# Quarter tiles for every attention product, source order on every queue, early loads on three queues

## The chip, the cores and the metric

The kernel runs on one core of one Trainium2 chip. The metric is device time in microseconds. The kernel before took 952.7 us, the median of three runs (951.31 to 954.98); one further execution was profiled, and every view below comes from it.

## The reference

Sigmoid attention over 8 batches, 12 heads, 448 positions and 64 values per head, then a top-1 mixture of experts over the 3584 tokens of 768 values (8 experts, 768 to 1024 to 768, fp32 throughout):

```python
def _attn_ref(q, k, v):                      # each (8, 12, 448, 64)
    scores = scale * np.matmul(q, k.transpose(0, 1, 3, 2)) - np.log(S)
    attn = 1.0 / (1.0 + np.exp(-scores))
    return np.matmul(attn, v)
...
x = attn_out.transpose(0, 2, 1, 3).reshape(B * S, H * D)      # (3584, 768)
def _moe_ref(x, w_gate, w1, w2):             # w1 (8, 768, 1024), w2 (8, 1024, 768)
    logits = x @ w_gate
    expert_idx = np.argmax(logits, axis=1)
    probs = softmax(logits)                  # sum + 1e-9
    gate_w = probs[np.arange(N), expert_idx]
    for e in range(E):
        mask = expert_idx == e
        h = np.maximum(x[mask] @ w1[e], 0.0)
        out[mask] = gate_w[mask, None] * (h @ w2[e])
```

## The kernel before

**Attention.** Two heads make a pair `g`, 6 pairs a batch, 48 in all. `load_pair` brings k and q of a pair in eight strided DMAs (32 partitions each), `turn` transposes them on VectorE (`kt`, `qt`: the two heads on partitions 0 to 63 and 64 to 127). `load_values` brings v. The 448 keys of a head are cut into three chunks of 128 keys and a rest of 64. For a chunk of 128, `scores` issues one matmul per head into a PSUM tile of its own (64 rows of the array by 128 columns: halves, line 492), `squash` turns each tile into sigmoids on ScalarE (line 478), and `weighted` multiplies them by v (128 rows by 64 columns: halves the other way, line 515). The rests of two pairs are put together: four matmuls on the four 64x64 quarters of the array (lines 500 and 524), the two heads of a pair into the two halves of one PSUM tile. Seven steps (3 + 3 chunks and one step of rests) do two pairs, so there are 168 steps. At each even step, called a visit here, TensorE does the value products of the two steps before (with exceptions at the ends of two pairs) and then the scores of two new steps. `xh` and `xl` (lines 530 and 531) take a finished pair out of PSUM as a sum of two parts.

**Experts.** The most frequent expert of each batch is applied to the whole batch in place (`moe`), with fp32 as a sum of two parts in three matmuls: 288 matmuls of 128x128 by 448 columns a batch (lines 208 and 229). `ps_moe` has two buffers, which the gate's small products share. `Weights.load` brings w1 in 8 and w2 in 6 tiles a batch (`wst`, five buffers), `part_split` makes the two parts of each: a cast on ScalarE (line 143) and a subtraction on GpSimd, called POOL (line 144). Tokens that chose another expert are done at the end, item by item, from `x_tok` and the records `recs` in DRAM.

**The mixture of both.** From step 33 on, 14 expert matmuls are written behind each step. The gate of a batch (`gate_a` to `gate_e`, `load_regs`) runs in steps 3 to 9 after the batch's attention; `tokens` writes `x_tok` in two halves through one buffer `xt` (lines 399 to 404), so the first transpose of the second half waits until the first half is written.

**Order.** Within `attention`, `manual_schedule(engines={ET.PE})` keeps TensorE's instructions in source order; VectorE and ScalarE are kept in source order only up to step 3. All else is ordered by a scheduler that works on a modelled time. Every queue executes in its order, and an instruction that waits holds what is behind it. After the attention the scheduler orders everything, in both kernels.

Of the kernel before, what the change touches and what calls it, by code (L numbers as in the profile page):

```python
# [25 lines left out]
def tile_sigmoid_attention_top1_moe(  # L26
# [78 lines left out]

    def setup():
        wg = const.tile([P, KD, E], F32, name="wg")
        nc.sync.dma_start(wg, w_gate.rearrange("(t p) e -> p t e", p=P))
        nc.scalar.copy(wgs[:, :, 0:E], wg)
# [152 lines left out]
    def gate_b(b):  # L262
# [29 lines left out]
        s1 = tl("s1")  # L292
        nc.scalar.activation(s1, z, AF.Sigmoid)
        s2 = tl("s2")
        nc.scalar.activation(s2, z, AF.Sigmoid, scale=-1.0)
        return oh, s1, s2

    def gate_c(b, oh, s1, s2):
# [121 lines left out]
    KC, KB = 3, 3 * P  # L420
# [24 lines left out]
    def load_values(g):  # L445
# [4 lines left out]
        t = apool.tile([P, 2, KC, D], F32, tag="vn", bufs=3, name=f"vn_{g}")  # L450
        eng.dma_start(t, v[b, 2 * hp : 2 * hp + 2, :KB].rearrange("h (p c) d -> p h c d", c=KC))
        e = apool.tile([P, D], F32, tag="ve", bufs=4, name=f"ve_{g}")
        for h in range(2):
            eng.dma_start(e[quarter(g, h)], v[b, 2 * hp + h, KB:, :])
        ops[g, "v"] = (t, e)

    def turn(g, nm):
# [15 lines left out]
    ST = 2 * KC + 1  # L473
    N_ST = NG // 2 * ST

    def squash(g, c, h, ps):
# [1 line left out]
        nc.scalar.activation(at, ps[:, :S], AF.Sigmoid, bias=bias_s, scale=SCALE)  # L478
# [5 lines left out]
    def scores(s):  # L484
        u, i = divmod(s, ST)
        n, c = divmod(i, KC)
        if n < 2:
            g = 2 * u + n
            pss = [score_tile(f"{g}_{c}_{h}") for h in range(2)]
            for h in range(2):  # L490
                ks = ops[g, "k"][OWN[h], :KB].rearrange("d (p c) -> d c p", c=KC)[:, c]
                nc.tensor.matmul(pss[h][:, :S], ks, ops[g, "q"][OWN[h]], start=True, stop=True)  # L492
            for h in range(2):
                squash(g, c, h, pss[h])
        else:
            pss = [score_tile(f"{2 * u + n}_{KC}") for n in range(2)]
            for n in range(2):
                g = 2 * u + n
                for h in range(2):
                    nc.tensor.matmul(  # L500
                        pss[n][quarter(g, h), :S], ops[g, "k"][OWN[h], KB:], ops[g, "q"][OWN[h]],
                        start=True, stop=True,
                    )
            for n in range(2):
                squash(2 * u + n, KC, 0, pss[n])

    def weighted(s):
        u, i = divmod(s, ST)
        n, c = divmod(i, KC)
        if n < 2:  # L510
            g = 2 * u + n
            if c == 0:
                psv[g] = ps_av.tile([P, 512], F32, tag="av", name=f"av_{g}")
            for h in range(2):
                nc.tensor.matmul(  # L515
                    psv[g][OWN[h], :S], ops[g, "v"][0][:, h, c, :], ats.pop((g, c, h)), start=(c == 0), stop=False
                )
            return
        for n in range(2):
            g = 2 * u + n  # L520
            at = ats.pop((g, KC, 0))
            for h in range(2):
                rows = quarter(g, h)
                nc.tensor.matmul(psv[g][OWN[h], :S], ops[g, "v"][1][rows], at[rows], start=False, stop=True)  # L524
        for n in range(2):
            g = 2 * u + n
            pv = psv.pop(g)
            xh = xpool.tile([P, S], F32R, tag="xh", name=f"xh_{g}")
            xl = xpool.tile([P, S], F32R, tag="xl", name=f"xl_{g}")
            nc.scalar.copy(xh, pv[:, :S])  # L530
            nc.vector.tensor_sub(xl, pv[:, :S], xh.bitcast(F32))  # L531
            xch[divmod(g, NP)] = (xh, xl)
# [4 lines left out]
    ET = mybir.EngineType
    ORDERED_TO = 3
# [382 lines left out]
```

## Time and profile before

| | |
|---|---|
| median of 3 runs | 952.7 us (951.31 to 954.98) |
| profiled execution, its own time | 959.16 us |
| its span, first to last instruction | 957.4 us |
| TensorE busy | 897.4 us (94%) |
| GpSimd (POOL), ScalarE (ACT), VectorE (DVE) busy | 407.2, 385.7, 350.1 us |
| mean granted TensorE clock | 0.970 |
| DMA | 120.47 MB, 319250 packets, of them 222596 under 512 B |
| first matmul of attention, first expert matmul | 8.06 us, 96.70 us |

How to read it: TensorE shows as PE (matmuls) and PEld (weight loads, which overlap them). A row of the timeline has a start, a length, an engine, a line, an operation with output and inputs, a count, and in brackets the idle time before it and what ended that. SPq, ACTq and POOLq are the queues on which SyncE, ScalarE and GpSimd issue DMAs. Matmuls are pipelined, so lengths of single matmuls overlap, and distances from start to start say more than lengths.

### The profile page before, as it was taken

The page shows a single profiled execution, that of the slowest core. Times are in us where ns is not written, and L with a number is a line of the kernel's source. Part 1 is how long each engine was busy: PE and PEld are TensorE (multiplying, and loading weights), DVE is VectorE, ACT ScalarE, POOL GpSimd, SP SyncE. Part 2 cuts the span into 40 slices and gives each one's busy share as a digit, 9 for nine tenths or more (in the row PEclk, how much of TensorE's full clock was granted, in tenths as well). Part 3 has the DMA queues.
Part 4 walks back from the last instruction along what each step waited for, and adds up shares of the span by engine and source line. Part 5 has one row for each costly group of instructions (what it writes and reads, how often), then busy time and mean ns, then how long its engine had stood idle before and what let it go on. Part 6 is the DMA issues. An engine that isn't in the chain of part 4 may idle for free.

```text
span 957.4 us, 13357 instructions
## 1 busy us (share of the span) xinstructions
PE 897.4 (94%) x4470; PEld 624.7 (65%) x4470; DVE 350.1 (37%) x730; ACT 385.7 (40%) x690; POOL 407.2 (43%) x362
## 2 busy tenths in 40 slices
PE   9778999999999999997999999999999999997986
PEld 5223667666656767665766766767666678996786
DVE  3335333621352324621334323513352325136354
ACT  4444453325233443343333633435343532313344
POOL 3002431835056523653047613743255508967130
PEclk9778999999999999998999999999999999998898
DMA  9667862755437653955347653946353405529414
GB/s 128 118 121 173 163 155 55 184 122 161 79 90 148 134 137 65 190 100 158 59 112 146 153 116 75 201 106 149 60 150 91 139 1 147 161 56 301 148 43 140
DMA packets 319250, 120.47 MB, mean 126 GB/s; under 512 B 222596, under 2 KB 314212, under 8 KB 319184
## 3 DMA queue, kind: packets, MB, share of 16 engines
q1 hardware_dynamic: 310512, 106.34, 48.2%
q0 software_dynamic: 6816, 13.07, 5.5%
q8 instruction: 35, 0.57, 0.3%
q10 hardware_dynamic: 1856, 0.23, 0.2%
q14 instruction: 31, 0.25, 0.1%
HBM read 97.55 MB, written 24.64 MB: 128 GB/s over the span
## 4 chain that ended last, share of the span: by engine, by line
PE 53%; DMA 7%; DVE 3%; issue 2%; ACT 2%; SPq 1%; POOL 1%; POOLq 0%; DVEq 0%; ACTq 0%
PE ps L229 18%; PE ps L208 12%; PE av L515 6%; PE sc L492 6%; PE ps L797 6%; DMA wst<-in_moe_w_dram 5%; PE psg L256 1%; PE sc L500 1%; PE av L524 1%; DMA x_tok<-xt 1%; DMA w2r<-in_moe_w_dram 1%; DMA w1r<-in_moe_w_dram 1%; SPq L439 1%; POOL w2l L144 0%; ACT w2h L143 0%
## 5 line engine op out<-in xcount | busy, mean ns | idle before, releaser
L478 ACT ACTIVATE at<-sc,bias_s 128x448 f32<-128x448 f32 x336 | 187.6, 636 | 234.9 <-PE sc L492 208.2
L144 POOL TENSOR_TENSOR w2l<-wst,w2h 128x512 fp32r<-128x512 f32 x96 | 123.9, 1307 | 279.1 <-ACT w2h L143 217.6
L144 POOL TENSOR_TENSOR w1l<-wst,w1h 128x768 fp32r<-128x768 f32 x64 | 117.2, 1841 | 158.5 <-ACT w1h L143 157.7
L229 PE MATMUL ps<-hh,w2h 128*128 128x448 f32 x384 | 144.1, 375 | 7.4 <-DVE gt L381 2.7
L208 PE MATMUL ps<-xh,w1h 128*128 128x448 f32 x384 | 142.9, 372 | 8.0 <-DVE hl L214 8.0
L492 PE MATMUL sc<-qt,kt 64*128 64x448 f32 x576 | 141.4, 598 | 5.8 <-ACT at L478 5.3
L515 PE MATMUL av<-at,vn 128*64 128x448 f32 x576 | 134.7, 582 | 12.2 <-DVE xl L531 11.1
L229 PE MATMUL ps<-hl,w2h 128*128 128x448 f32 x384 | 143.4, 373 | 0.0
L229 PE MATMUL ps<-hh,w2l 128*128 128x448 f32 x384 | 142.1, 370 | 0.6 <-POOL w2l L144 0.6
L208 PE MATMUL ps<-xl,w1h 128*128 128x448 f32 x384 | 142.1, 370 | 0.0
L208 PE MATMUL ps<-xh,w1l 128*128 128x448 f32 x384 | 141.8, 369 | 0.0
L492 PEld LDWEIGHTS sc<-qt,kt 64*128 64x128 f32 x576 | 67.7, 254 | 84.1 <-issue 63.1
L214 DVE SCALAR_TENSOR_TENSOR hl<-ps,hh 128x448 fp32r<-128x448 f32 x64 | 39.8, 622 | 196.6 <-ACT hh L213 196.6
L143 ACT CAST w2h<-wst 128x512 fp32r<-128x512 f32 x96 | 57.6, 621 | 99.4 <-PE ps L229 58.7
L229 PEld LDWEIGHTS ps<-hh,w2h 128*128 128x128 f32 x384 | 75.0, 195 | 21.4 <-issue 9.0
L208 PEld LDWEIGHTS ps<-xh,w1h 128*128 128x128 f32 x384 | 72.3, 188 | 23.6 <-DVE hl L214 10.0
L515 PEld LDWEIGHTS av<-at,vn 128*64 128x64 f32 x576 | 37.4, 142 | 76.5 <-issue 52.0
L229 PEld LDWEIGHTS ps<-hh,w2l 128*128 128x128 f32 x384 | 75.0, 195 | 12.0 <-issue 5.5
L229 PEld LDWEIGHTS ps<-hl,w2h 128*128 128x128 f32 x384 | 75.0, 195 | 9.7 <-issue 6.2
L143 ACT CAST w1h<-wst 128x768 fp32r<-128x768 f32 x64 | 53.5, 836 | 68.8 <-DMA wst<-in_moe_w_dram 25.1
L208 PEld LDWEIGHTS ps<-xh,w1l 128*128 128x128 f32 x384 | 72.1, 188 | 13.2 <-issue 7.5
L208 PEld LDWEIGHTS ps<-xl,w1h 128*128 128x128 f32 x384 | 72.4, 189 | 12.6 <-issue 7.1
(148 smaller groups left out, 907.7 us busy)
## 6 DMA issues: line engine op xcount, KB each, us to landing
wst<-in_moe_w_dram SPq DMA_DIRECT2D x64, 384.0 KB
wst<-in_moe_w_dram SPq DMA_DIRECT2D x48, 512.0 KB
kn<-in_k_dram SPq DMA_DIRECT2D x192, 56.0 KB
x_tok<-xt SPq DMA_DIRECT2D x64, 168.0 KB
out_dram<-ob POOLq DMA_DIRECT2D x96, 112.0 KB, 3.2
qn<-in_q_dram SPq DMA_DIRECT2D x188, 56.0 KB
vn<-in_v_dram SPq DMA_DIRECT2D x45, 192.0 KB
w1r<-in_moe_w_dram SPq DMA_DIRECT2D x12, 512.0 KB
```

The costliest lines, as they stand in the source:

```text
L143: nc.scalar.copy(hi, st)
L144: eng.tensor_tensor(lo, st, hi.bitcast(F32), op=ALU.subtract)
L208: nc.tensor.matmul(ps[:, :S], a[:, ws], b_, start=(t == 0 and n == 0), stop=(t == KD - 1 and n == 2))
L214: nc.vector.scalar_tensor_tensor(hl[:, :S], ps[:, :S], 0.0, hh[:, :S].bitcast(F32), op0=ALU.max, op1=ALU.subtract)
L229: nc.tensor.matmul(ps[:, :S], a, b_, start=(j == 0 and n == 0), stop=(j == KF - 1 and n == 2))
L256: nc.tensor.matmul(psg[: 2 * E, :S], wgs[:, t], xch[b, t][n], start=(t == 0 and n == 0), stop=(t == KD - 1 and n == 1),)
L439: eng.dma_start(t[32 * a : 32 * (a + 1)], src[b, 2 * hp + h, :, 32 * f : 32 * (f + 1)].rearrange("(j r) s -> r j s", r=32),)
L478: nc.scalar.activation(at, ps[:, :S], AF.Sigmoid, bias=bias_s, scale=SCALE)
L492: nc.tensor.matmul(pss[h][:, :S], ks, ops[g, "q"][OWN[h]], start=True, stop=True)
L500: nc.tensor.matmul(pss[n][quarter(g, h), :S], ops[g, "k"][OWN[h], KB:], ops[g, "q"][OWN[h]], start=True, stop=True,)
L515: nc.tensor.matmul(psv[g][OWN[h], :S], ops[g, "v"][0][:, h, c, :], ats.pop((g, c, h)), start=(c == 0), stop=False)
L797: nc.tensor.matmul(*a, **kw)
```

## The change

Every attention product becomes a quarter. The 448 keys of a head are cut into seven chunks of 64 (`KC = S // DK`). A step takes one chunk of two pairs: four score matmuls on the four quarters into two PSUM tiles, two sigmoids, and later four value matmuls on the quarters. Seven steps still do two pairs. v of a pair comes in two DMAs, one per head, with seven consecutive keys on a partition.

All engines, and the queues of DMAs with them, are in source order while the attention lasts. The order of loads and transposes within seven steps (`READY`) is rewritten, `kt`, `qt` and `vn` have four buffers where they had three. The first expert's weights are loaded where they were, but cast at step 32 (`ahead(0)`, then `ahead(2)`).

Loads: q of pairs 0 and 1 on ScalarE's queue (before: pair 0), v of pairs 0 to 9 on POOL's (before: 0 to 2), the gate weights and the blank of `recs` on POOL's (before: SP's). The gate weights' cast and subtraction move from ScalarE and VectorE to POOL. The gate's two small sigmoids move from `gate_b` to `gate_c`, one step later.

```diff
+    wg = const.tile([P, KD, E], F32, name="wg")
     def setup():
-        nc.sync.dma_start(wg, w_gate.rearrange("(t p) e -> p t e", p=P))
-        nc.scalar.copy(wgs[:, :, 0:E], wg)
-        nc.vector.tensor_sub(wgs[:, :, E : 2 * E], wg, wgs[:, :, 0:E].bitcast(F32))
+        nc.gpsimd.tensor_copy(wgs[:, :, 0:E], wg)
+        nc.gpsimd.tensor_sub(wgs[:, :, E : 2 * E], wg, wgs[:, :, 0:E].bitcast(F32))
...
-        nc.sync.dma_start(recs.rearrange("(p r) w -> p r w", p=P), blank3)
+        nc.gpsimd.dma_start(recs.rearrange("(p r) w -> p r w", p=P), blank3)
...
-    KC, KB = 3, 3 * P
+    DK = P // 2
+    KC = S // DK
...
-            eng = nc.scalar if (g, nm) == (0, "q") else nc.sync
+            eng = nc.scalar if g < Q_ACT and nm == "q" else nc.sync
...
-        t = apool.tile([P, 2, KC, D], F32, tag="vn", bufs=3, name=f"vn_{g}")
-        eng.dma_start(t, v[b, 2 * hp : 2 * hp + 2, :KB].rearrange("h (p c) d -> p h c d", c=KC))
-        e = apool.tile([P, D], F32, tag="ve", bufs=4, name=f"ve_{g}")
+        t = apool.tile([P, KC, D], F32, tag="vn", bufs=4, name=f"vn_{g}")
         for h in range(2):
-            eng.dma_start(e[quarter(g, h)], v[b, 2 * hp + h, KB:, :])
-        ops[g, "v"] = (t, e)
+            eng.dma_start(t[quarter(g, h)], v[b, 2 * hp + h].rearrange("(p c) d -> p c d", c=KC))
+        ops[g, "v"] = t
...
     def scores(s):
+        u, c = divmod(s, ST)
+        two = [2 * u + n for n in range(2)]
+        pss = [score_tile(f"{g}_{c}") for g in two]
+        for g, ps in zip(two, pss):
             for h in range(2):
+                ks = ops[g, "k"][OWN[h]].rearrange("d (p c) -> d c p", c=KC)[:, c]
+                nc.tensor.matmul(ps[quarter(g, h), :S], ks, ops[g, "q"][OWN[h]], start=True, stop=True)
+        for g, ps in zip(two, pss):
+            squash(g, c, ps)
...
-    WARM, V_POOL = 76, 3
+    WARM, V_POOL, Q_ACT = 76, 10, 2
...
     READY = {
-        0: lambda u: (turn(2 * u + 1, "k"), load_values(2 * u + 1)),
-        1: lambda u: turn(2 * u + 1, "q"),
-        2: lambda u: load_pair(2 * u + 5),
-        4: lambda u: (turn(2 * u + 2, "k"), load_values(2 * u + 2)),
-        5: lambda u: (turn(2 * u + 2, "q"), load_pair(2 * u + 6)),
+        0: lambda u: (turn(2 * u + 2, "k"), load_pair(2 * u + 4)),
+        1: lambda u: (turn(2 * u + 2, "q"), load_values(2 * u + 2)),
+        3: lambda u: (turn(2 * u + 3, "k"), load_pair(2 * u + 5)),
+        4: lambda u: (turn(2 * u + 3, "q"), load_values(2 * u + 3)),
     }
...
-        order.enter_context(tc.manual_schedule(engines={ET.PE}))
-        first = order.enter_context(ExitStack())
-        first.enter_context(tc.manual_schedule(engines={ET.DVE, ET.Activation}))
+        order.enter_context(tc.manual_schedule())
...
+            if s == START - 1:
+                wts.ahead(2)
...
-                        wts.ahead(2)
+                        wts.ahead(0)
```

Three places show what moves. On TensorE, early in the attention before, around the first step of rests: `sc` rows of 128x448 are halves, `sc` rows of 64x448 quarters, `av` rows from `vn` halves and from `ve` quarters.

```order
L515 MATMUL av_368<-at_0_0_306,vn_284 64x448
L515 MATMUL av_368<-at_0_1_308,vn_284 64x448
L515 MATMUL av_368<-at_1_0_329,vn_284 64x448
L515 MATMUL av_368<-at_1_1_331,vn_284 64x448
L500 MATMUL sc_3_373<-qt_229,kt_227 64x448 x2
L500 MATMUL sc_3_374<-qt_289,kt_282 64x448 x2
L492 MATMUL sc_0_0_383<-qt_348,kt_341 128x448
L492 MATMUL sc_0_1_384<-qt_348,kt_341 128x448
```

The same place in the changed kernel: a visit of two value steps and two score steps.

```order
L503 MATMUL av_298<-at_1_277,vn_230 64x448 x2
L503 MATMUL av_301<-at_1_279,vn_237 64x448 x2
L503 MATMUL av_298<-at_2_310,vn_230 64x448 x2
L503 MATMUL av_301<-at_2_312,vn_237 64x448 x2
L490 MATMUL sc_4_344<-qt_228,kt_226 64x448 x2
L490 MATMUL sc_4_345<-qt_235,kt_233 64x448 x2
L490 MATMUL sc_5_354<-qt_228,kt_226 64x448 x2
L490 MATMUL sc_5_355<-qt_235,kt_233 64x448 x2
```

Three shapes in a visit have become one. On ScalarE before, at the place of the gate weights and then at that of the first expert's weights (`at` are sigmoids, `xh` copies of finished pairs, `w1h` casts):

```order
L478 ACTIVATE at_2_0_424<-sc_2_0_420,bias_s 128x448
L109 CAST wgs<-wg 128x6x8
L478 ACTIVATE at_2_1_426<-sc_2_1_421,bias_s 128x448
...
L143 CAST w1h_0_853<-wst_0_843 128x768
L530 CAST xh_903<-av_684 128x448
L530 CAST xh_907<-av_752 128x448
L143 CAST w1h_1_859<-wst_1_845 128x768
L478 ACTIVATE at_2_0_915<-sc_2_0_911,bias_s 128x448
```

and the changed kernel's ScalarE at the first expert's weights:

```order
L511 CAST xh_975<-av_740 128x448
L511 CAST xh_979<-av_743 128x448
L477 ACTIVATE at_2_989<-sc_2_983,bias_s 128x448
L477 ACTIVATE at_2_991<-sc_2_984,bias_s 128x448
L477 ACTIVATE at_3_999<-sc_3_993,bias_s 128x448
L477 ACTIVATE at_3_1001<-sc_3_994,bias_s 128x448
L143 CAST w1h_0_1025<-wst_0_924 128x768
L143 CAST w1h_1_1031<-wst_1_926 128x768
```

The cast of the gate weights has left ScalarE, and the copies of the finished pairs stand ahead of the first expert cast. On VectorE before, `xf` and `xt` are the token transposes of batch 0, and `xt_1` opens the second half:

```order
L399 TENSOR_TENSOR xf_1_0_1064<-xh_540,xl_541 128x448
L462 STREAM_TRANSPOSE kt_635<-kn_430 128x448
L462 STREAM_TRANSPOSE qt_672<-qn_435 128x448
L462 STREAM_TRANSPOSE kt_719<-kn_493 128x448
L462 STREAM_TRANSPOSE qt_773<-qn_498 128x448
L400 STREAM_TRANSPOSE xt_1_1063<-xf_1_0_1064 128x14x32
L531 TENSOR_TENSOR xl_649<-av_570,xh_648 128x448
```

and in the changed kernel, where `hl` is the second part of the first expert's hidden values:

```order
L399 STREAM_TRANSPOSE xt_0_1021<-xf_0_2_1093 128x14x32
L214 SCALAR_TENSOR_TENSOR hl_0_1144<-ps_0_0_1085,hh_0_1143 128x448
L398 TENSOR_TENSOR xf_1_0_1158<-xh_584,xl_585 128x448
L399 STREAM_TRANSPOSE xt_1_1157<-xf_1_0_1158 128x14x32
L461 STREAM_TRANSPOSE kt_1175<-kn_905 128x448
L398 TENSOR_TENSOR xf_1_1_1187<-xh_707,xl_708 128x448
L399 STREAM_TRANSPOSE xt_1_1157<-xf_1_1_1187 128x14x32
L214 SCALAR_TENSOR_TENSOR hl_0_1144<-ps_0_1_1153,hh_0_1143 128x448
```

The tokens of batch 0 have moved from the first stage to steps 31 to 36, among the first expert's hidden values.

More of the change, by code (lines that the diff above doesn't have):

```diff
@@ L104, in tile_sigmoid_attention_top1_moe @@
     wgs = const.tile([P, KD, 2 * E], F32R, name="wgs")
+    wg = const.tile([P, KD, E], F32, name="wg")
     def setup():
-        wg = const.tile([P, KD, E], F32, name="wg")
-        nc.sync.dma_start(wg, w_gate.rearrange("(t p) e -> p t e", p=P))
-        nc.scalar.copy(wgs[:, :, 0:E], wg)
-        nc.vector.tensor_sub(wgs[:, :, E : 2 * E], wg, wgs[:, :, 0:E].bitcast(F32))
+        nc.gpsimd.tensor_copy(wgs[:, :, 0:E], wg)
+        nc.gpsimd.tensor_sub(wgs[:, :, E : 2 * E], wg, wgs[:, :, 0:E].bitcast(F32))
         blank = wpool.tile([P, 1024], U32, tag="wst", bufs=RAWS_AHEAD, name="blank")
@@ L291, in gate_b, with gate_c @@
         nc.vector.tensor_tensor(z, lg, bc(mx), op=ALU.subtract)
[L292 to L298, printed above, removed]
+        return oh, z
+    def gate_c(b, oh, z):
         def tl(nm, shape, dt=F32):
             return small.tile(shape, dt, tag=nm, name=f"{nm}_{b}")
+        s1, s2 = tl("s1", [P, NCH, E]), tl("s2", [P, NCH, E])
+        nc.scalar.activation(s1, z, AF.Sigmoid)
+        nc.scalar.activation(s2, z, AF.Sigmoid, scale=-1.0)
         pc = small_ps(b, "pc")
@@ L460, in turn @@
             return
-        t = apool.tile([P, S], F32, tag=nm + "t", bufs=3, name=f"{nm}t_{g}")
+        t = apool.tile([P, S], F32, tag=nm + "t", bufs=4, name=f"{nm}t_{g}")
         nc.vector.transpose(t, ops.pop((g, nm + "n")).rearrange("p j s -> p (j s)"))
@@ L471, in tile_sigmoid_attention_top1_moe, with squash @@
     ats, psv = {}, {}
-    ST = 2 * KC + 1
+    ST = KC
     N_ST = NG // 2 * ST
-    def squash(g, c, h, ps):
-        at = apool.tile([P, S], F32, tag="at", bufs=10, name=f"at_{g}_{c}_{h}")
+    def squash(g, c, ps):
+        at = apool.tile([P, S], F32, tag="at", bufs=10, name=f"at_{g}_{c}")
         nc.scalar.activation(at, ps[:, :S], AF.Sigmoid, bias=bias_s, scale=SCALE)
-        ats[g, c, h] = at
+        ats[g, c] = at
     def score_tile(name):
@@ L484, in scores @@
     def scores(s):
[L485 to L489, printed above, removed]
-            for h in range(2):
[L491 to L505, printed above, removed]
+        u, c = divmod(s, ST)
@@ L510, in weighted @@
-        if n < 2:
-            g = 2 * u + n
+        u, c = divmod(s, ST)
+        two = [2 * u + n for n in range(2)]
+        for g in two:
             if c == 0:
                 psv[g] = ps_av.tile([P, 512], F32, tag="av", name=f"av_{g}")
[L514 to L521, printed above, removed]
+            at = ats.pop((g, c))
@@ L522, in weighted @@
             for h in range(2):
                 rows = quarter(g, h)
[L524 to L532, printed above, removed]
@@ L534, in tile_sigmoid_attention_top1_moe @@
-    WARM, V_POOL = 76, 3
+                nc.tensor.matmul(
+                    psv[g][OWN[h], :S], ops[g, "v"][rows, c, :], at[rows], start=(c == 0), stop=(c == KC - 1)
+                )
+        if c == KC - 1:
+            for g in two:
+                pv = psv.pop(g)
+                xh = xpool.tile([P, S], F32R, tag="xh", name=f"xh_{g}")
+                xl = xpool.tile([P, S], F32R, tag="xl", name=f"xl_{g}")
+                nc.scalar.copy(xh, pv[:, :S])
+                nc.vector.tensor_sub(xl, pv[:, :S], xh.bitcast(F32))
+                xch[divmod(g, NP)] = (xh, xl)
@@ L557, in attention @@
         load_pair(1)
-        turn(0, "k")
-        turn(0, "q")
-        load_values(0)
-        for g in (2, 3, 4):
+        for g in range(2):
+            turn(g, "k")
+            turn(g, "q")
+            load_values(g)
+        for g in (2, 3):
             load_pair(g)
+        nc.gpsimd.dma_start(wg, w_gate.rearrange("(t p) e -> p t e", p=P))
         pend_gate = None
@@ L568, in attention @@
                 setup()
-            if s == ORDERED_TO:
-                first.close()
+            if s == START - 1:
+                wts.ahead(2)
             if s % 2 == 0:
```

4 lines of the change are left out of this document (removed).

## The prediction

> **What bounds the kernel now.** I read the busy times by stage first, because the share of the whole span mixes three stages with different limits. The first row ends at the first expert matmul, the second at the end of the attention work. The columns are the stretch, its length, busy us (and count) of PE, PEld, DVE, ACT, POOL, then granted clock, DMA share and GB/s.
>
> ```profile
> 0.00:96.70 96.70, 77.68 (x389) 33.31 (x390) 35.05 (x91) 43.88 (x82) 14.69 (x31) 0.86 0.75 136
> 96.70:797.00 700.30, 679.27 (x3323) 465.04 (x3321) 244.83 (x505) 284.57 (x514) 309.65 (x261) 0.99 0.53 120
> 797.00:957.40 160.40, 140.41 (x761) 126.33 (x760) 70.24 (x134) 57.29 (x96) 82.87 (x72) 0.94 0.46 144
> ```
>
> In the long middle stage TensorE is idle for 700.30 - 679.27 = 21.0 us only, at a full clock, and no other engine passes 45%: that stage is bound by TensorE, so it gets shorter only if the matmuls take fewer slots. In the first stage TensorE is idle for 19 us and its clock is 0.86. That stage has stops in it. The third stage holds no instruction that the change writes differently.
>
> Next, the timeline of the first stage, for the three long stops of TensorE and for what stood in their way (start, length, instruction, count, idle before it and its releaser).
>
> ```profile
> 32.86 0.23 ACT L109 CAST wgs<-wg 128x48 fp32r<-128x48 f32 x1 [7.22 <-DMA wg<-in_moe_w_gate_dram]
> 33.68 1.86 PE L492 MATMUL sc<-qt,kt 64*128 64x448 f32 x2 [5.27 <-ACT at L478]
> 64.75 0.65 DVE L400 STREAM_TRANSPOSE xt<-xf 128x448 f32<-128x448 f32 x1 [8.06 <-DMA x_tok<-xt]
> 65.96 3.26 PE L515 MATMUL av<-at,vn 128*64 128x448 f32 x8 [6.93 <-DVE xl L531]
> 88.11 0.83 ACT L143 CAST w1h<-wst 128x768 fp32r<-128x768 f32 x1 [3.68 <-DMA wst<-in_moe_w_dram]
> 90.09 4.75 PE L515 MATMUL av<-at,vn 128*64 128x448 f32 x12 [3.88 <-DVE xl L531]
> 96.70 0.47 PE L208 MATMUL ps<-xh,w1h 128*128 128x448 f32 x1
> ```
>
> Each stop is an in-order queue standing behind a transfer: ScalarE behind the gate weights (TensorE idle 5.27), VectorE behind the write of x_tok (6.93), ScalarE behind the first expert weights (3.88). What follows each, in the columns of the first fence:
>
> ```profile
> 33.60:40.70 7.10, 7.02 (x18) 2.02 (x22) 0.00 (x0) 2.33 (x6) 0.00 (x0) 0.50 0.60 113
> 65.90:71.40 5.50, 5.44 (x14) 1.96 (x16) 2.98 (x6) 0.30 (x1) 0.00 (x0) 0.50 0.63 116
> 90.00:95.30 5.30, 5.21 (x14) 1.75 (x16) 3.27 (x7) 3.39 (x6) 4.21 (x5) 0.50 1.15 239
> ```
>
> The granted clock is half there: the x8 at 65.96 takes 3.26, the same x8 below 1.72. Half of 7.1 + 5.5 + 5.3 is 9 us lost beside 16.1 us of idle time, so the stops cost about 25 us.
>
> Last, how attention matmuls sit on TensorE in the middle stage. One fp32 matmul shows as two records. A "slot" is what fills the array once: two halves (x4) or four quarters (x8).
>
> ```profile
> 99.74 2.48 PE L515 MATMUL av<-at,vn 128*64 128x448 f32 x12
> 102.14 0.98 PE L500 MATMUL sc<-qt,kt 64*64 64x448 f32 x8
> ...
> 345.62 1.72 PE L515 MATMUL av<-at,vn 128*64 128x448 f32 x8
> 347.27 1.09 PE L492 MATMUL sc<-qt,kt 64*128 64x448 f32 x4
> 348.29 0.98 PE L500 MATMUL sc<-qt,kt 64*64 64x448 f32 x8
> 349.20 0.47 PE L208 MATMUL ps<-xh,w1l 128*128 128x448 f32 x1
> ...
> 355.07 0.97 PE L515 MATMUL av<-at,vn 128*64 128x448 f32 x4
> 355.97 0.98 PE L524 MATMUL av<-at,ve 64*64 64x448 f32 x8
> 356.88 1.84 PE L492 MATMUL sc<-qt,kt 64*128 64x448 f32 x8
> 358.65 0.47 PE L208 MATMUL ps<-xh,w1h 128*128 128x448 f32 x1
> ```
>
> Start to start, value halves take 0.90 for one slot (355.07 to 355.97), 1.65 for two, 2.40 for three: 0.75 a slot and 0.15 once for a run of one shape. Score halves take 1.02 for one and 1.77 for two: 0.75 and 0.27. One slot of quarters takes 0.91: 0.75 and 0.16. So a change of tile shape costs 0.15 to 0.27, and a visit to attention (two steps) has two or three of them.
>
> **Quarters.** The number of slots stays: 7 for scores and 7 for values per two pairs. What goes is changes of shape. Per 14 steps (seven visits) scores now take 5 x 1.77 + 2 x (1.02 + 0.91) = 12.71, and values, whose visits hold 2, 2, 2, 2, 1, 3 and 2 steps, take 4 x 1.65 + (0.90 + 0.91) + 0.91 + 2.40 = 11.72; sum 24.43. After, values and scores of a visit follow each other in one shape: 28 x 0.75 + 7 x 0.16 = 22.12. That is 2.31 per 14 steps, 0.165 a step, and 135 of the 168 steps lie in the TensorE-bound stage: **-22.3 us**. No row shows two slots of quarters in a row, nor values followed by scores in one shape. Bounds: if a change between values and scores still costs 0.16, the gain is 0.165 - 0.08 a step, 11.5 us; if every slot of quarters costs the 0.91 of a lone one, 28 x 0.91 = 25.5 against 24.43 is a loss of 10 us. I take the upper gain, because the same two passes stream in halves and quarters, and the halves' further slots cost 0.75 in all three run lengths. The Trainium skill (TensorEngine Tiling (Array Packing), Key Properties) says that changing the tiling mode, not just the tile, drains the array; that agrees with the 0.15 to 0.27 per change of shape.
>
> ScalarE's sigmoids keep number and shape (seven of 128x448 per pair), and so do the evictions. TensorE gets 28 matmuls of each kind where 16 were; the L500 row shows eight records in 0.98, so their issue hides under the streaming.
>
> **The first stage, rebuilt.** Rows for its terms:
>
> ```profile
> 5.61 0.65 DVE L462 STREAM_TRANSPOSE kt<-kn 128x448 f32<-128x448 f32 x1 [2.72 <-DMA kn<-in_k_dram]
> 8.06 1.84 PE L492 MATMUL sc<-qt,kt 64*128 64x448 f32 x8
> 9.28 0.65 DVE L462 STREAM_TRANSPOSE kt<-kn 128x448 f32<-128x448 f32 x1 [2.49 <-DMA kn<-in_k_dram]
> 12.14 0.65 DVE L462 STREAM_TRANSPOSE qt<-qn 128x448 f32<-128x448 f32 x1 [2.22 <-DMA qn<-in_q_dram]
> 20.07 1.99 SPq L439 DMA_DIRECT2D qn<-in_q_dram  x4
> 51.20 2.21 ACT L478 ACTIVATE at<-sc,bias_s 128x448 f32<-128x448 f32 x4 [1.75 <-PE sc L492]
> 71.94 0.38 PE L256 MATMUL psg<-xh,wgs 128*16 128x448 f32 x1
> 74.20 0.37 PE L256 MATMUL psg<-xl,wgs 128*16 128x448 f32 x1
> 82.23 0.15 DVE L313 TENSOR_SCALAR ri<-cr 128x1 int32<-128x1 f32 x1
> 84.62 3.93 SPq L165 DMA_DIRECT2D wst<-in_moe_w_dram  x5
> 89.03 1.82 POOL L144 TENSOR_TENSOR w1l<-wst,w1h 128x768 fp32r<-128x768 f32 x1 [80.34 <-ACT w1h L143]
> vn<-in_v_dram POOLq DMA_DIRECT2D x3, 192.0 KB, 4.0
> ve<-in_v_dram POOLq DMA_DIRECT2D x6, 16.0 KB, 5.0
> ```
>
> The first visit now needs both pairs. k of pair 1 lands at 9.28; q of pair 1 moves from SP, where it lands at 12.14, to ScalarE's queue behind q of pair 0, so it lands between those two. I take 10.0 and 0.6 for its transpose: scores flow at 10.6, not 8.06. Then 34 score and 31 value slots to the first expert matmul, 65 x 0.75 = 48.8, with 0.16 for each of 17 visits 51.5; the gate's twelve matmuls take 2.5 (71.94 to 74.4) and its small ones with their waits another 2.5. The expert weights: from the gate's counts to the expert number some 2 (a matmul and six small VectorE operations like that at 82.23, an estimate), 2.4 to the issue (82.23 to 84.62), 3.5 to the cast (88.11), 0.83 and 1.82 for the two parts, 10.5 in all, against three visits of four slots, 3.2 each, that TensorE still has; I take 2 us of wait. Sum 10.6 + 51.5 + 5 + 2 = 69.1 against 96.70: **-27.6 us**.
>
> What keeps the stops away: the gate weights' load, cast and subtraction go to POOL, where only value loads of pairs 4 and 5 stand behind them, which no matmul needs before step 14. x_tok's halves are made in source order, at steps 31 to 36, so nothing in the first 30 steps stands behind their write. The first two expert casts stand behind the copies of the preceding av, not ahead of them.
>
> What must hide: four DMAs of q or k take 1.99 on SP, 4.0 a pair, and the values' three DMAs leave that queue; a pair has 3.5 steps of 1.58 (22.12 / 14) on TensorE, 5.5. The eight q issues on ScalarE end before its first sigmoid can start. ScalarE's 2.21 of sigmoids fit a visit of 3.2. The value loads wait on POOL for the buffer of the pair four back, then two pairs take four issues, 2.0 at SP's rate, and 4 to 5 to land, 7, against six steps, 9.5; if that cover fails, 2 or 3 us at each of three turns. Bounds of this stage: 64 with no weights' wait and q at 9.3, and 81 (the transfer rival below), so -16 to -33.
>
> **Source order in the middle stage.** A wait on any queue now holds all that is written after it. These are the waits there already (total, times, longest):
>
> ```profile
> PE ps L208 <- DVE hl L214: 8.0, 5, 4.8
> DVE xt L400 <- DMA x_tok<-xt: 36.7, 8, 8.1
> ACT s L293 <- DVE z L291: 18.4, 5, 7.2
> ```
>
> In each batch the fourth token transpose must wait until the first half of x_tok is written, one step after that write is issued (14 expert matmuls at 0.21, since 28 fill 349.20 to 355.07, and 1.58: 4.5 us), and on SP the write stands behind eight q and k loads (4 us). VectorE waits there already, 4.6 on average, and TensorE pays 8 us for hl in all. The two small sigmoids move one step later, so that ScalarE need not stand at z. The weights' loads keep their distance of five tiles. I take +6 us; the bounds are -10 (half of the 21 us idle goes) and +40 (5 us a batch).
>
> **Sum.** The profiled execution took 959.16 us, 6.5 above the median of 952.7. 959.2 - 27.6 - 22.3 + 6 = 915.3. Other runs lie lower and the profile does not say where; I take half the difference off: **912 us**.
>
> **Rivals.** The page's second part, the busy tenths of the DMA engines in 40 slices of 24 us:
>
> ```profile
> DMA  9667862755437653955347653946353405529414
> ```
>
> (a) The first stage is bound by transfers. Its DMA share is 0.75 over 96.7 us, 72.5 us of full use; at the nine tenths of the first slice the first expert matmul comes at 81: 12 us more, 924. For it: the wait for kn at 9.28. Against: x_tok's writes leave the stage. The Trainium skill (Trainium Kernel Development and Optimization, Key Constraints) says that queues on several engines share the same 16 DMA engines and that spreading saves issue time only; the trace agrees so far that SP issues without pause early on, 4.1 us a pair. (b) Quarters keep 0.91 a slot: the 22.3 turns into +10, 947; or only the seam between values and scores stays, 923. (c) Slower: VectorE behind x_tok. If the wait per batch reaches 14 us, it passes the 7 us that the second PSUM buffer covers (18 expert matmuls, 3.8, and a visit, 3.2), TensorE stands 7 us and runs 3.4 us at half clock, eight times: some 70 us, 982. It decides from about 12 us, half as much again as the longest wait now, 8.1. (d) Both quarters of a pair write one PSUM tile. If two row halves of the array could not write the same bank together, a slot would take 1.5, and 168 steps of 3.0 against 1.75 would add 210 us, 1125. The L500 row speaks against it: four such quarters take 0.91. This is the rule of the Trainium skill (TensorEngine Tiling (Array Packing), Gotcha 1: PSUM Pressure), that different row tiles cannot access one bank simultaneously; the trace does not show its price. (e) The steady waits grow by 20 to 40 us without deciding: 930 to 950.
>
> **Chances.** Forecast, 895 to 928: 0.60. (a) 0.12, (b) 0.09, (e) 0.10, (c) 0.07, (d) 0.02. The range 890 to 942 leaves out (c), (d), the full (b) and the end of (e), and on the low side a first stage of 64 with less idle time than now. Within 0.5% of 952.7, which is what a measurement can tell, or slower is left to (c), (d) and the tail of (b) and (e): faster 0.88, same 0.04, slower 0.08.
>
> **What would show it.** Right: the first L208 near 69 us; no stop over 3 us before it except at 8 to 10.6; quarters with 0.75 from slot to slot and no gap between av and sc; a middle stage near 135 steps times 0.165 shorter. Wrong: av to sc still 0.9, kt or xt waiting over 10 us for a DMA, or PE waiting for hl by tens of us.

## The result, and the profile after

The changed kernel takes **911.2 us** (median of 4 runs, 909.5 to 911.6); the kernel before took 952.6 beside it. The ratio is 0.9559, 95% interval 0.9537 to 0.9581. The forecast was 912. The sum was right and three of its terms were not. Among the runs of the next section, two slow executions are left out: one with source order on TensorE and VectorE (975.0 us), and the profiled one with source order on TensorE and ScalarE (1415.6 us at a granted clock of 0.556), which is why that kernel has no stages in the table.

The profiled execution took 911.15 us, its span is 908.9. Busy times by stage, in the columns of the prediction's first fence; the stages end at the first visit with both pairs, at the first expert matmul, at the last attention product (the prediction's second row ran on from there, to 797.0) and at the end of the experts' work in place, and the last holds the items:

```profile
0.00:13.40 13.40, 7.28 (x80) 6.46 (x80) 3.53 (x11) 2.12 (x3) 8.75 (x27) 0.95 1.08 151
13.40:74.65 61.25, 58.70 (x538) 33.26 (x538) 26.92 (x69) 41.21 (x77) 11.68 (x18) 0.93 0.85 148
74.65:725.80 651.15, 638.53 (x4189) 455.92 (x4185) 255.18 (x498) 278.60 (x509) 302.42 (x253) 1.00 0.58 131
725.80:829.40 103.60, 95.38 (x443) 85.73 (x442) 48.91 (x93) 29.06 (x45) 70.98 (x64) 0.93 0.50 140
829.40:908.90 79.50, 61.70 (x383) 54.52 (x380) 37.70 (x59) 31.36 (x57) 20.73 (x16) 0.90 0.37 126
```

The kernel before, cut at the same places from its first expert matmul (96.70) on:

```profile
96.70:784.50 687.80, 666.77 (x3263) 454.57 (x3261) 238.57 (x496) 281.11 (x508) 300.97 (x253) 0.99 0.54 121
784.50:878.70 94.20, 91.23 (x441) 82.28 (x442) 38.80 (x84) 29.38 (x45) 70.78 (x63) 0.98 0.50 147
878.70:957.40 78.70, 61.68 (x383) 54.51 (x381) 37.70 (x59) 31.36 (x57) 20.77 (x16) 0.90 0.37 127
```

So the first stage became 22.1 us shorter and the middle 36.6; the experts behind the attention became 9.4 longer. The rows of the changed kernel's timeline that answer to those in the prediction, first the start and then one visit:

```profile
12.19 0.65 DVE L461 STREAM_TRANSPOSE kt<-kn 128x448 f32<-128x448 f32 x1 [5.16 <-DMA kn<-in_k_dram]
13.41 2.52 PE L490 MATMUL sc<-qt,kt 64*64 64x448 f32 x10 [4.97 <-DVE qt L461]
...
74.65 0.47 PE L208 MATMUL ps<-xh,w1h 128*128 128x448 f32 x1
...
96.12 2.49 PE L503 MATMUL av<-at,vn 64*64 64x448 f32 x24
98.42 1.68 PE L490 MATMUL sc<-qt,kt 64*64 64x448 f32 x16
100.04 0.47 PE L208 MATMUL ps<-xl,w1h 128*128 128x448 f32 x1
```

Three slots of values take 2.30 from start to start, two of scores 1.62: 0.77 and 0.81 a slot, the change to the experts' shape included, with nothing between av and sc. The three long stops of the first stage are gone; a new one of 4.97 stands at its start, and the granted clock is 0.50 from there to 18.9.

Behind the attention there are two stops that the kernel before did not have. TensorE's rows with what follows each, then VectorE's and POOL's there:

```profile
761.79 0.47 PE L208 MATMUL ps<-xh,w1l 128*128 128x448 f32 x1 [1.88 <-POOL w1l L144]
763.24 0.57 PE L208 MATMUL ps<-xh,w1l 128*128 128x448 f32 x1
777.89 0.74 PE L208 MATMUL ps<-xh,w1h 128*128 128x448 f32 x1 [3.73 <-DVE hl L214]
778.43 0.58 PE L208 MATMUL ps<-xl,w1h 128*128 128x448 f32 x1
```

```profile
760.66 5.01 DVE L398 TENSOR_TENSOR xf<-xh,xl 128x448 f32<-128x448 f32 x1
776.68 0.65 DVE L399 STREAM_TRANSPOSE xt<-xf 128x448 f32<-128x448 f32 x1 [4.43 <-DMA x_tok<-xt]
758.92 0.98 POOL L355 DMA_INDIRECT recs<-rec,si  x1 [0.30 <-issue]
759.91 3.62 POOL L144 TENSOR_TENSOR w1l<-wst,w1h 128x768 fp32r<-128x768 f32 x2
763.47 1.71 POOL L239 TENSOR_TENSOR ob<-ob,gt 128x896 f32<-128x896 f32 x1
```

w1l stands behind the scatters of the records, hl behind an xt that waits for x_tok. Matmuls of 0.57 in place of 0.37 show the half clock after each: it lasts from 762.9 to 766.2 and from 777.9 to 783.3. The two stops (1.88 and 3.73) and half of these 8.7 us make 10 us, an estimate from these rows, against the 9.4 that the stage grew.

### The profile page after: what moved, and what is told of

It is laid out like the page before. It is cut to its first block, busy times and chain, and to the rows that moved or that the text cites. A ratio compares the mean times of both kernels' runs of the same rounds, so it can differ in the third digit from the quotient of the medians.

```text
span 908.9 us, 15548 instructions
## 1 busy us (share of the span) xinstructions
PE 861.6 (95%) x5622; PEld 635.9 (70%) x5622; DVE 372.2 (41%) x729; ACT 382.4 (42%) x689; POOL 414.6 (46%) x377
## 4 chain that ended last, share of the span: by engine, by line
PE 82%; DVE 6%; DMA 3%; POOL 3%; issue 2%; SPq 1%; ACT 1%; POOLq 0%; ACTq 0%; DVEq 0%
PE ps L208 24%; PE ps L229 22%; PE av L503 14%; PE sc L490 13%; PE ps L775 6%; PE psg L256 2%; DMA x_tok<-xt 1%; DMA qn<-in_q_dram 1%; POOL w1l L144 1%; DVE xf L398 1%; SPq L403 1%; DVE ob L237 1%; POOL out_dram L244 1%; POOL ob L239 1%; DMA out_dram<-ob 1%
## 5 line engine op out<-in xcount | busy, mean ns | idle before, releaser
L144 POOL TENSOR_TENSOR w1l<-wst,w1h 128x768 fp32r<-128x768 f32 x64 | 119.5, 1880 | 136.0 <-ACT w1h L143 131.2
L490 PE MATMUL sc<-qt,kt 64*64 64x448 f32 x1344 | 153.0, 544 | 5.0 <-DVE qt L461 5.0
L503 PE MATMUL av<-at,vn 64*64 64x448 f32 x1344 | 155.6, 555 | 0.1
L490 PEld LDWEIGHTS sc<-qt,kt 64*64 64x64 f32 x1344 | 77.2, 191 | 65.3 <-issue 55.1
L214 DVE SCALAR_TENSOR_TENSOR hl<-ps,hh 128x448 fp32r<-128x448 f32 x64 | 39.5, 617 | 187.1 <-ACT hh L213 186.9
L503 PEld LDWEIGHTS av<-at,vn 64*64 64x64 f32 x1344 | 49.0, 134 | 61.3 <-issue 50.4
L213 ACT ACTIVATE hh<-ps 128x448 fp32r<-128x448 f32 x64 | 35.2, 551 | 95.9 <-PE ps L208 95.9
```

The costliest lines, as they stand in the source:

```text
L144: eng.tensor_tensor(lo, st, hi.bitcast(F32), op=ALU.subtract)
L213: nc.scalar.activation(hh[:, :S], ps[:, :S], AF.Relu)
L214: nc.vector.scalar_tensor_tensor(hl[:, :S], ps[:, :S], 0.0, hh[:, :S].bitcast(F32), op0=ALU.max, op1=ALU.subtract)
L490: nc.tensor.matmul(ps[quarter(g, h), :S], ks, ops[g, "q"][OWN[h]], start=True, stop=True)
L503: nc.tensor.matmul(psv[g][OWN[h], :S], ops[g, "v"][rows, c, :], at[rows], start=(c == 0), stop=(c == KC - 1))
```

## The experiments

Ratios are to the kernel before on the same chip, with their 95% intervals; the stages are those of each kernel's profiled execution. The kernel before took 952.6 to 957.8 us beside the different groups of runs, so between two rows a difference of a few us is safer read from the ratios.

| kernel | us | ratio | to first expert matmul | middle | experts behind |
|---|---|---|---|---|---|
| before | 952.6 | 1 | 96.7 | 687.8 | 94.2 |
| changed | 911.2 | 0.956 (0.954-0.958) | 74.7 | 651.2 | 103.6 |
| halves put back | 926.7 | 0.969 (0.964-0.974) | 71.7 | 673.4 | 104.4 |
| before with quarters alone | 976.3 | 1.019 (1.013-1.026) | 106.2 | 696.5 | 95.6 |
| source order: PE | 964.2 | 1.008 (1.005-1.011) | 96.9 | 689.8 | 97.3 |
| source order: PE, DVE | 960-969 | 1.011 (1.002-1.020) | 81.3 | 691.2 | 106.9 |
| source order: PE, ACT | 919-925 | 0.965 (0.959-0.971) | | | |
| source order: PE, DVE, ACT | 916.5 | 0.956 (0.950-0.962) | 73.8 | 663.9 | 104.4 |
| loads back on SyncE | 917.1 | 0.959 (0.954-0.964) | 79.1 | 652.2 | 104.2 |
| longer warm-up | 912.0 | 0.951 (0.945-0.958) | 71.1 | 654.8 | 103.8 |
| two xt buffers | 901.3 | 0.939 (0.933-0.945) | 74.1 | 649.5 | 98.3 |
| + last batch rearranged | 909.0 | 0.949 (0.943-0.955) | 73.9 | 649.2 | 106.4 |
| + another start | 905.9 | 0.948 (0.942-0.954) | 70.8 | 649.1 | 103.5 |
| two xt buffers, other start | 901.6 | 0.942 (0.939-0.946) | 72.4 | 650.1 | 98.3 |

**The shapes.**

```diff
-    KC = S // DK           # 7 chunks of 64, all quarters
+    KC, KB = 3, 3 * P      # scores, weighted, load_values of the kernel before
```

> The changed kernel with the old tile shapes put back: halves for three chunks and quarters for the fourth, three transfers for a pair's values. Source order and the spread loads stay. Theory 1 (the shapes are worth what the slots say): 0.165 us a step come back, 168 steps, 27.7 us, so 939 us (933 to 944); the middle stage is longer by 20 to 24 us with TensorE as idle as in the changed kernel (about 13 us), and visits take 3.3 to 3.6 us again instead of 3.17. Theory 2 (the order of the queues made the gain, and the quarters only came with it): 911 to 918 us. Theory 3 (quarters also make queues wait less, since two pairs advance together): over 945 us, with TensorE's idle time in the middle near 21 us.

Measured 926.7. The row of its middle stage:

```profile
71.70:745.10 673.40, 661.79 (x3263) 455.04 (x3261) 253.28 (x498) 280.77 (x509) 305.13 (x254) 0.99 0.55 126
```

TensorE is idle 11.6 us there, 12.6 in the changed kernel, and the stage is 22.2 longer: theory 1 for the middle. In the first stage the halves are 3.0 us better: pair 0 alone keeps TensorE at work from the start (its longest stop in the first 22 us is 0.84, its clock in the stage 1.00). So the whole, 15.5 us by time and 12 by ratio, lies between the ranges of theories 1 and 2; the profiled executions, 928.0 against 908.9 in span, differ by 19.1.

**Quarters without the order.**

```diff
 # in the kernel before: scores, weighted, load_values, READY of the changed one
-        for g in (2, 3, 4):
+        for g in (2, 3):
```

> The kernel before with the quarters alone (and the turns of both next pairs in the loop, which quarters need); its scheduling and its loads stay. Theory 1 (the parts add): 27.7 us off 952.6, so 925 us (920 to 931), with the three stops of the first stage still there. Theory 2 (all by order): 945 to 953. Theory 3 (quarters need both pairs early, and with the old queues the transfers of the first stage come too late): the first expert matmul at 95 us or later, 930 to 940.

976.3, slower than the 957.5 of the kernel before beside it. None of the theories allowed for that. The middle stage:

```profile
106.20:802.70 696.50, 656.98 (x4187) 464.18 (x4185) 241.81 (x494) 279.28 (x507) 297.86 (x251) 0.98 0.53 118
```

TensorE is busy 9.8 us less there than in the kernel before, but its idle time grew from 21.0 to 39.5 us (696.50 less 656.98). Which engine held which was the next question.

**Whose order.** The scheduler was put back by engine:

```diff
-        order.enter_context(tc.manual_schedule())
+        order.enter_context(tc.manual_schedule(engines={ET.PE}))   # DVE, ACT to step 3
+        ... {ET.PE, ET.DVE}   /   {ET.PE, ET.Activation}   /   {ET.PE, ET.DVE, ET.Activation}
```

> The changed kernel with the scheduler put back: source order for TensorE, and for VectorE and ScalarE until step 3 only. Quarters and spread loads stay. Theory A (source order took stops out of the middle stage, some 15 us, and the x_tok stop out of the first, 7 to 10 us, and gave 9 us back at the end): 911 + 23 - 9 = 925 us (918 to 932), TensorE's idle time in the middle stage near 21 us again, and the expert work behind the last attention near 94 us instead of 103.6. Theory B (the forecast's: source order costs 6 us of steady waits): 903 to 908 us. Theory C (order is worth nothing either way): 911 +- 4.

> The changed kernel with source order on TensorE and VectorE alone; ScalarE, GpSimd and SyncE go by the scheduler again. The scheduler on all but TensorE took 964 us, source order on all 911. Theory A (it is VectorE's order: hl stood behind an xt that waited for x_tok, 18.3 us of TensorE's idle time in the middle, and half clock after it): 920 to 932 us, TensorE's waits for hl in the middle under 6 us, and no x_tok stop in the first stage; what is left is the stop for sigmoids behind the first expert casts on ScalarE, 4 us and half clock. Theory B (ScalarE's order decides: casts ahead of sigmoids and of xh): 945 to 960 us. Theory C (the order of the transfers on SyncE decides, x_tok's writes above all): 950 to 964, with xt waiting 40 us for x_tok as before and hl still late.

> The changed kernel with source order on TensorE, VectorE and ScalarE; GpSimd and SyncE go by the scheduler. Theory A (the two queues that only issue transfers, scatters and subtractions follow the others anyway): 911 us (907 to 916). Theory B (the scheduler's places of x_tok's writes and of the weights' loads on SyncE cost as much as the compute engines' order): 920 to 940. Theory C (source order on these two costs: POOL's scatters ahead of a w1l at 759.9 in the last batch): 905 to 909.

> The changed kernel with source order on TensorE and ScalarE alone; VectorE, GpSimd and SyncE go by the scheduler. So far: TensorE alone 964, with VectorE 965, with VectorE and ScalarE 916.5, all 911. Theory A (ScalarE's order alone decides: the scheduler puts casts, whose weights have not landed, ahead of hh, xh and sigmoids): 914 to 925 us, TensorE's waits for hl in the middle under 8 us. Theory B (both orders are needed, since VectorE by the scheduler has xt ahead of hl): 930 to 950, with the x_tok stop of 6 us in the first stage and hl stops of 10 us or more in the middle.

With quarters, source order is worth 53 us by time and 50 by ratio, nearly four times the 14 of theory A of the first. VectorE's order by itself shortens the first stage (96.9 to 81.3), lengthens that of the experts behind the attention (97.3 to 106.9) and gives nothing in all: 960 to 969, at and above the upper ends of theories B and C. ScalarE's gives nearly all: 919 to 925, theory A in time, though its waits were not seen at full clock. Both give 916.5 (the stages in the table are those of its slowest execution, 922.4), and the order of SyncE and GpSimd is within the error by ratio, 0.956 with and without. The waits (total, times, longest), first of the kernel before, then of PE alone, of PE with DVE, and of the changed kernel:

```profile
ACT w2h L143 <- DMA wst<-in_moe_w_dram: 36.8, 22, 4.4
ACT w1h L143 <- DMA wst<-in_moe_w_dram: 25.1, 17, 5.8
```

```profile
ACT w2h L143 <- DMA wst<-in_moe_w_dram: 56.1, 21, 5.5
ACT w1h L143 <- DMA wst<-in_moe_w_dram: 46.2, 18, 9.8
DVE xt L399 <- DMA x_tok<-xt: 40.2, 8, 12.2
PE ps L208 <- DVE hl L214: 18.3, 6, 5.9
```

```profile
ACT w2h L143 <- DMA wst<-in_moe_w_dram: 66.3, 22, 6.5
ACT w1h L143 <- DMA wst<-in_moe_w_dram: 45.9, 19, 8.0
DVE xt L399 <- DMA x_tok<-xt: 17.0, 7, 6.1
PE ps L208 <- DVE hl L214: 26.5, 9, 7.8
```

```profile
DVE xt L399 <- DMA x_tok<-xt: 41.2, 8, 10.8
PE ps L208 <- DVE hl L214: 6.7, 3, 3.7
ACT w1h L143 <- DMA wst<-in_moe_w_dram: 4.7, 3, 3.7
```

x_tok is no help in telling them apart: xt waits 17 us where TensorE waits 26.5 for hl, and 41 where it waits 6.7. ScalarE's casts are of help: they stand 102 and 112 us before weights that have not landed, 62 before the change, 5 after. The longest stop of the PE and DVE kernel, in its rows of ScalarE, VectorE, TensorE and SyncE:

```profile
414.56 1.14 ACT L143 CAST w2h<-wst 128x512 fp32r<-128x512 f32 x2 [6.15 <-DMA wst<-in_moe_w_dram]
421.56 1.14 ACT L143 CAST w2h<-wst 128x512 fp32r<-128x512 f32 x2 [4.26 <-DMA wst<-in_moe_w_dram]
422.60 0.52 ACT L511 CAST xh<-av 128x448 fp32r<-128x448 f32 x1
425.27 0.62 ACT L143 CAST w2h<-wst 128x512 fp32r<-128x512 f32 x1 [1.61 <-DMA wst<-in_moe_w_dram]
428.08 0.56 ACT L213 ACTIVATE hh<-ps 128x448 fp32r<-128x448 f32 x1
428.67 0.62 DVE L214 SCALAR_TENSOR_TENSOR hl<-ps,hh 128x448 fp32r<-128x448 f32 x1 [2.77 <-ACT hh L213]
429.35 0.74 PE L208 MATMUL ps<-xh,w1h 128*128 128x448 f32 x1 [7.79 <-DVE hl L214]
409.16 11.22 SPq L136 DMA_DIRECT2D wst<-in_moe_w_dram  x3
```

The scheduler put casts of later weights ahead of xh, the sigmoids and hh, and the casts wait for loads, of which SyncE issues three in 11.22 us (last row). hh waits, hl waits for hh, TensorE for hl. TensorE's wait carries VectorE's name and has ScalarE's cause. Why the scheduler's places cost more with quarters than with halves (113 us of such waits with quarters alone) was not tried, and neither was an order undone engine by engine with halves: that ScalarE decides there too is argued from its 62 us.

**The loads.**

```diff
-    WARM, V_POOL, Q_ACT = 76, 10, 2
+    WARM, V_POOL, Q_ACT = 76, 3, 1     # and wg, recs on nc.sync
```

> The changed kernel with the loads put back on SyncE: q of pair 1, the values from pair 3 on, the gate weights and the blank records. The cast of the gate weights stays on GpSimd, source order stays. Theory A (spreading saves issue time only, and only where SyncE is behind: the start): q of pair 1 lands 2 to 4 us later, so the first full visit starts at 15 to 17 instead of 13.4, the rest as it was: 914 us (911 to 918). Theory B (the old queue is what made the waits of the first stage): stops of 3 us or more come back before the first expert matmul: 920 to 932. Theory C (more transfers on SyncE delay x_tok's writes, and VectorE and TensorE behind them): the middle stage grows by 10 us or more, 925 and over.

917.1, in theory A's range, though at another place than it said: the first full visit starts earlier (12.7), and it is the values, on SyncE behind k and q, that come late:

```profile
29.89 1.64 PE L503 MATMUL av<-at,vn 64*64 64x448 f32 x5 [2.27 <-DMA vn<-in_v_dram]
```

The first expert matmul is 4.5 us later, the middle 1 us longer. By ratio the loads are worth 3 us, with overlapping intervals.

**The start.**

```diff
-    WARM, V_POOL, Q_ACT = 76, 10, 2
+    WARM, V_POOL, Q_ACT = 166, 10, 2
```

> The changed kernel with 166 warm-up matmuls in place of 76, so that TensorE works until just before q of pair 1 has been turned, rather than stand from 8.45 to 13.41 us; nothing else moves. Theory A (TensorE runs at half clock from 13.4 to 18.9 because it stood 5 us): the first visits run at 0.75 us a slot at once, the first expert matmul comes 2.0 to 3.0 us sooner than 74.65, the whole at 908 us (906 to 910). Theory B (the half clock there has another cause, the start of the fp32 work or the transfers): first expert matmul at 74.6 +- 0.5, 911 us. Theory C (the longer warm-up ends too late): up to 1 us slower.

The clock is as theory A says: 1.00 over the first stage. The time is not. TensorE's rows:

```profile
13.80 1.40 PE L490 MATMUL sc<-qt,kt 64*64 64x448 f32 x10 [0.80 <-DVE qt L461]
...
71.11 0.47 PE L208 MATMUL ps<-xh,w1h 128*128 128x448 f32 x1
...
73.41 0.47 PE L208 MATMUL ps<-xh,w1l 128*128 128x448 f32 x1 [1.64 <-POOL w1l L144]
73.72 0.36 PE L208 MATMUL ps<-xh,w1h 128*128 128x448 f32 x1
```

The first expert matmul is 3.5 us sooner, and the third waits 1.64 for the low part of its weights. Of the other 1.9 us, 1.6 are lost between 347 and 368 us, matmul compared with matmul, and the end is the same: 908.7 against 908.9 in span. That loss is no wait. Both kernels have the same stop there, for the gate's gm; the first two rows are from the kernel with the longer warm-up, the others from the changed one:

```profile
358.14 0.37 PE L378 MATMUL pg<-gm,same 128*128 128x16 f32 x2 [1.86 <-DVE gm L374]
359.31 0.57 PE L229 MATMUL ps<-hl,w2h 128*128 128x448 f32 x1
360.31 0.36 PE L378 MATMUL pg<-gm,same 128*128 128x16 f32 x2 [1.85 <-DVE gm L374]
361.02 0.36 PE L229 MATMUL ps<-hh,w2l 128*128 128x448 f32 x1
```

Half clock follows in the one and not in the other. The gain of 3.5 holds the reverse: a stop of 1.63 for gm in the first stage was followed by half clock in the changed kernel (0.51 from 70 to 72) and by full clock here; 1.85 us were gained before it. So the start is worth some 2 us, of which the wait for w1l takes 1.6, and the clock after short stops moves the time by as much again.

**x_tok.**

```diff
-xts[b] = xtpool.tile([P, NB, KH, 32], F32, tag="xt", bufs=1, ...)
+xts[b] = xtpool.tile([P, NB, KH, 32], F32, tag="xt", bufs=2, ...)   # at: bufs 10 -> 8
```

> The changed kernel with two buffers for xt (and eight instead of ten for the sigmoids' outputs, which makes the room), so that VectorE no longer waits for x_tok's first half to be written. Theory A (VectorE behind x_tok costs where no attention covers it, in the last batch: 3.73 us of stop and 3.4 us lost at half clock, and some 3 in the middle): 901 to 906 us, the expert work behind the last attention 97 to 99 us instead of 103.6. Theory B (the wait is hidden, another one takes its place, the expert casts or w1l): 908 to 912. Theory C (eight buffers for the sigmoids' outputs are too few): slower than 913.

Theory A: 901.3. (The two fewer buffers of at were not tried by themselves.) xt's 41 us of waits are gone, the experts behind the attention take 5.3 us less:

```profile
723.60:821.90 98.30, 91.61 (x441) 82.14 (x442) 52.66 (x93) 29.06 (x45) 70.43 (x64) 0.98 0.52 147
759.58 0.47 PE L208 MATMUL ps<-xh,w1l 128*128 128x448 f32 x1 [1.88 <-POOL w1l L144]
```

The stop for hl falls from 3.73 to 1.76 us; what is left of it stands behind a sum xf that takes 5.93 (at 765.90). The stop for w1l is 1.88 as before, but no half clock follows it (granted clock 1.00 from 759.5 to 770). In the changed kernel it lasted 3.3 us; half of that, some 1.6 of the 5.3, is therefore not shown to be xt's.

**The last batch, and both.**

```diff
+                if b == B - 1:
+                    at = ("a", "b", "c", "l", None, "e") + (None,) * 8 + ("d",)
+                t0 = 1 if b == B - 1 else 7      # tokens six steps earlier
```

> The kernel with two xt buffers (901.25 us), and in the last batch the tokens six steps earlier (beside the previous batch's second matrix, where VectorE has no hl to make) and the scatters of the records ten steps later (after most w1l subtractions). Theory A (behind the last attention TensorE waits for w1l behind POOL's scatters, 2.5 us, and for hl behind xf, 1.8, and runs at half clock for some us after each): 898.3 less 4 to 5, so 896 to 899 with the expert work behind the last attention at 94 to 95 us instead of 98.3. Theory B (the expert weights' transfers, which all eight raw tiles wait for, are late anyway): w1l waits stay, 900 to 902. Theory C (the scatters now collide with later subtractions): 902 to 905.

None of the theories: 8 us slower than without it, by ratio 0.949 against 0.939 with intervals that just overlap, and 8.1 us longer in the stage that the change is about. TensorE's stops for the batch's first expert parts stay (rows below), one for the item list comes (ki, behind the gate's late counts, 2.7 us), and the one for ob grows from 2.1 to 3.9:

```profile
755.68 0.47 PE L208 MATMUL ps<-xh,w1h 128*128 128x448 f32 x1 [1.28 <-ACT w1h L143]
757.58 0.50 PE L208 MATMUL ps<-xh,w1l 128*128 128x448 f32 x1 [1.22 <-POOL w1l L144]
```

```diff
+        eng = nc.gpsimd if 2 <= g < V_POOL else nc.sync
+    WARM, V_POOL, Q_ACT = 120, 10, 2
+            if s == 0:                            # setup(), was s == 6
```

> The kernel before this one with another start: the values of the first two pairs go to SyncE behind k of pair 1, the gate weights' cast and the blank records come before the values of pairs 2 and 3 on GpSimd, and 120 warm-up matmuls stand where 76 were. Theory A (q and k of pair 1 land late because the values share the transfer engines): pair 1 lands 2 to 3 us sooner, TensorE goes from the warm-up to the first visit with under 2 us of stop and at full clock, the first expert matmul comes at 70 to 72 us and the whole gains 2 to 4 us over the kernel without it: 893 to 896. Theory B (a start gained is lost again, as with the longer warm-up alone, since w1l of the first expert comes when its chain from the gate lets it): within 1 us of the kernel without it. Theory C (the later values of pair 0 and 1 stop the first value products): slower by 1 to 3 us.

The start came 3.0 us sooner in the profile and the time 3.1, inside the intervals. Then the two that paid, without the rearranged last batch:

> The two changes that paid, together: two xt buffers (901.25 us), and the other start (the values of pairs 0 and 1 on SyncE behind k of pair 1, the gate weights and blank records ahead of the later values on GpSimd, 120 warm-up matmuls), which brought the first expert matmul from 73.85 to 70.83 and 3.1 us in all. The last batch is as in the changed kernel. Theory A (the two add): 898 us (895 to 901), the first expert matmul at 70.8, the expert work behind the last attention at 98 us. Theory B (the start is lost to the w1l wait of the first expert, 1.6 us, and later stops): 900 to 902.

901.6: theory B. The first expert matmul comes at 72.39 and the next but one waits 1.64 for w1l. So the two xt buffers are what is left: 901.3 us, 10 under the changed kernel, and intervals of the ratios that do not overlap (0.933 to 0.945 against 0.954 to 0.958).

## Why the prediction was right, and where it was not

- **Quarters, -22.3: right.** With order and loads fixed, the middle moves by 22.2 us (673.4 to 651.2), and the rivals (b) and (d) fall: 0.77 a slot with both row halves writing one bank. The upper gain was taken for the right reason, the slot spacing of halves: five slots in one shape take 3.92 (2.30 and 1.62), where 0.75 a slot and 0.16 a visit make 3.91.
- **The first stage, -27.6: mis-sized by 5.5.** The first full visit was put at 10.6 and came at 13.41, since k of pair 1 landed at 12.19 and not at 9.28: the DMA engines are busy throughout there (share 1.08 up to 13.4), and where the values of the first two pairs were moved behind that k (the last kernel of the table) it landed at 9.46. That is 2.8 us. And the half clock after the stop was not priced, though the prediction had priced it for the old stops: from 13.4 to 18.9, half of 5.5, 2.7 us by estimate. Little of the two was won back by an earlier start, because the first expert's w1l then came late, as the longer warm-up showed.
- **Source order, +6: wrong in sign.** Order and loads together, with halves, move the middle by -14.4 (687.8 to 673.4); the loads moved it by 1 at most with quarters. The step that failed is the choice of waits. It looked at VectorE (x_tok, z), priced steady waits, and read ScalarE's stand before unlanded weights only in the first stage, where it called it a stop. The list of waits had it for the whole span, 62 us in 39 waits, under ScalarE's name. The wait that it did price came nearly as said and cost little: xt waited 41.2 us where it had waited 36.7, once 10.8, over the 10 that the prediction called a sign of being wrong, and TensorE's waits for hl went from 8.0 to 6.7.
- **The third stage, 0: wrong, +9.4.** It was costed at nothing because no line in it is written differently. The tokens, scatters and casts of the last batch are in source order too, and no attention covers them there. For the hl stop this is the mechanism of rival (c), in one place instead of eight, and the order is VectorE's: the stage is 97.3 with TensorE alone in source order and 106.9 with VectorE added. What the scatters ahead of w1l cost is not shown by itself: with GpSimd and SyncE left to the scheduler that stop goes, another of 6.34 us for gm (at 768.98) comes, and the stage stays at 104.4.
- **The sum.** -22.1 - 36.6 + 9.4 + 0.8 for the items gives 48.5 off the span; forecast was 43.9 off the profiled execution and 3.3 off for the median's distance. The misses cancelled, which is luck: 911.2 against 912 says less for the reasoning than it seems.
- **Additivity** was not stated and did not hold: quarters alone cost 19 us (976.3 against 957.5 beside it), quarters after the order gain 12 to 15.

## What to carry to other kernels

A wait is caused by the engine at the far end of its chain: TensorE stood for VectorE, VectorE for ScalarE, ScalarE for a transfer, and only an order undone engine by engine showed which one to move. When an order is fixed for a whole kernel, look first at what stands before unlanded data with work behind it that another engine needs, and then at the stage with least cover. Two changes that each look like a gain in the profile are measured apart and together: here the quarters lost time before the order was fixed and gained time after. And a gain of one or two us is compared stop by stop, since half clock may or may not follow the same stop.

## What the runs showed of the hardware

A sum of two SBUF tiles on VectorE (xf) took 5.01 us at 760.66, in the changed kernel. It ended at 765.67, just behind POOL's w1l and ob (759.91 to 765.18). Where no sum of POOL's ran beside it, it took 0.58 to 0.63; the longest, 6.70 at 166.10, stood beside three w1l. The Trainium skill (SBUF — State Buffer, SBUF: two separate sides) says that VectorE and GpSimd share a pair of ports under an exclusive lock, which a VectorE operation with two SBUF inputs needs against a GpSimd operation that reads SBUF; the trace agrees.

The half clock does not follow from a stop's length alone. In the changed kernel it followed stops of 1.88 us (at 759.91; 0.57 a matmul at 763.24) and 1.63 (at 67.08; granted clock 0.51 from 70 to 72), and not one of 1.85 (before 360.31). In other kernels the same three stops did the opposite: 1.88 with two xt buffers and 1.63 with the longer warm-up were followed by full clock, 1.86 with the longer warm-up by half. The Trainium skill (TensorE: Matmul & The Clock Gate, What's actually happening) gives a free-running window of some 3.4 us and a drop after at least one idle window; here, of six stops of about half a window, three were enough and three were not, so a whole window of idle time was not needed. What decides besides the length, no run here shows.
